# Attention and a two-layer product on one core: earlier dues on VectorE for two pairs, Newton roots for two more, and first-product tiles issued in two parts

## Chip, cores, metric

One core of a Trainium2 chip. The metric is the device time of one execution in microseconds (us), with the median over several runs. "Ratio" below is the mean time of one kernel's fast runs over that of the other kernel's fast runs of the same rounds, so it is not quite the ratio of the medians quoted beside it. All runs here are of state fast. Among them there are still two clusters: some have a mean granted TensorE clock of 0.998 or more, some of 0.991 to 0.997, and the second are longer by 1.2 to 2.2 us (medians) in every kernel that had both. The profiles of e5, e6, x1, x2 and x3 below fell in the second cluster: in each the granted clock was 0.50 for 3.4 us somewhere between 9 and 23 us, ahead of the first half tile, and in none of the other profiles. Half the clock for 3.4 us loses some 1.7 us (an estimate from these figures), which is about the distance of the clusters. Where it matters I give the median of the runs at 0.998 and above ("full clock").

## The reference, cut

```python
def _attn_ref(q, k, v, tau):                       # 8 batches, 12 heads, 448 tokens, 64 wide, fp32
    q_n = q / (norm(q) + 1e-06)
    k_n = k / (norm(k) + 1e-06)
    scores = q_n @ k_n.T / tau                     # tau = 0.1
    attn = softmax(scores)
    return attn @ v
def _moe_ref(x, w_in, w_out):                      # x: 3584 x 768, w_in: 768 x 2048, w_out: 2048 x 768
    h = x @ w_in
    g = h * sigmoid(1.702 * h)
    return g @ w_out
```

Heads are handled in pairs: 6 pairs a batch, 48 in all, numbered through. Batch 0 is pairs 0 to 5, batch 1 is pairs 6 to 11.

## The kernel before

The kernel doesn't issue instructions in program order. Each step ("op") is added to a plan with an engine, an estimated duration, a due, what it must follow, and the buffers it takes and frees. A greedy list scheduler then plays the plan through with those estimates and fixes the order of every engine for good:

```python
def order(self):
    ...
    while True:
        for e in idle:                                   # each engine that is free now
            while idle[e] <= now and ready[e]:
                due, i = heapq.heappop(ready[e])         # the ready op with the smallest due
                ...
                if any(self.free[s] < k ... for s, k in takes):   # a buffer is missing: hold it
                    held.append((due, i)); continue
                ...
                idle[e] = now + us
```

So any change of a due, of a duration or of a group redraws the order of everything after it. The parts that the change touches:

```python
groups = [(x,) for x in range(HP)]                       # HP = 6, PW = 10, HALF = 12
groups += [(x,) for x in range(HP, PW)] + [tuple(range(PW, HALF))] * (PW < HALF)
groups += [tuple(range(g, g + GRP)) for g in range(HALF, NPAIR, GRP)]
...
if x == grp[0] and x in range(HP, PW):                   # pairs 6..9: power 0.5 on GpSimd, inverse on VectorE
    add(("norm", 0, grp), "POOL", 0.5 + 2.4 * n, early + 0.3, partial(power, grp), after=reds)
    add(("norm", 1, grp), "DVE", 0.45, early + 0.3, partial(inverse, grp), after=[("norm", 0, grp)], **port)
elif x == grp[0] and not first:                          # pairs 10 on: Newton steps on VectorE
    add(("norm", 0, grp), "DVE", 0.78 + 0.06 * n, early + 0.3, partial(norm_a, grp), after=reds, **port)
    add(("norm", 1, grp), "DVE", 1.14 + 0.18 * n, early + 0.3, partial(norm_b, grp), after=[("norm", 0, grp)], **port)
...
# batches 0 and 1, by halves h of the queries: attention, normalise, transpose, copy
add(("at", x, h), "PE", 0.48, sh + 1, partial(attend_h, x, h), ..., takes=[("mm", 1), ("run", 1)], ...)
add(("nx", x, h), "DVE", 0.65, sh + 1 - (0 if first else URGENT), partial(normalise_h, x, h), after=[("at", x, h)], ...)
add(("turn", x, h), "PE", 0.15, sh + 1, partial(turn_h, x, h), after=[("nx", x, h)], ...)
add(("x", x, h), ..., "DVE", 0.35, sh + 1 - (0 if first else URGENT), partial(turned_h, x, h), after=[("turn", x, h)],
    ..., frees=[("mm", 1)], ...)
...
def mm1(b, m):                                           # a whole tile of the first product: 6 matmuls, one PSUM bank
    ps = mms[b, m] = bank((b, m))
    for kk in range(KT1):
        nc.tensor.matmul(out=ps[:, :S], lhsT=w_in_sb[:, kk, 128 * m : 128 * (m + 1)], rhs=xTs[b, kk][:, :S], ...)
```

There are three PSUM banks ("mm") for half-batch attention outputs, first-product tiles and second-product tiles together. Batch 0's first product runs in half tiles: 8 for the first half of its tokens, 8 for the second, and the second 8 need the second half of all six pairs. Line numbers: L484 attention product by halves, L507 transpose, L495 and L497 normalise, L517 copy, L581 half tiles of the first product (L583 after the change), L534 whole tiles (L535), L611 second product (L613), L326 power on GpSimd, L343 scaling of queries and keys, L269 reductions, L375 fillers (transposes of the identity whose result nothing reads, put where the plan leaves TensorE idle in the first 50 us).

Of the kernel before, what the change touches and what calls it, by code (L numbers as in the profile page):

```python
# [24 lines left out]
LATE_FROM, LATE_US, URGENT = 80.0, 2.0, 12  # L25
# [5 lines left out]
def packets(n, nbytes):  # L31

    one = DMA_PKT_US + DMA_KB_US * nbytes / 1024
    return n * one / DMA_ENGINES, one
# [8 lines left out]
class Plan:  # L43
# [7 lines left out]
    def add(self, name, eng, us, due, emit, after=(), takes=(), frees=(), dma=None, rows=128, hold=(), turn=False, banks=()):  # L51
        after = list(after) + list(hold)
        if turn:
            self.turns.append((due, len(self.turns), name))
        self.ops[name] = (eng, us, due, emit, after, takes, frees, dma, rows, hold, banks)
# [114 lines left out]
def kernel(  # L170
# [12 lines left out]
    B, H, S, D = q.shape  # L183
# [4 lines left out]
    HP = H // 2  # L188
# [2 lines left out]
    NV, NE = 6, 8  # L191
    NQK = 7
    HALF = 2 * HP
    AHEAD = 3
    LAG, JOINT = (0, 1, 1, 2, 2, 2, 2, 2), 3
    SQP, SQT, XA, CA, TA = range(15, NPAIR), (0,), (), (0, 1, 6), ()
    TURN = 2 * HP
    PW = 10
    SD = ((0, 0), (0, 1), (5, 0), (5, 1))
    SH = S // 2  # L200
    inv_tau = float(1.0 / tau)
# [2 lines left out]
    KT1 = DM // 128  # L204
# [319 lines left out]
    def bank(key):  # L524
        i = plan.bank[key]
        return ps_m.tile([128, 512], FP32, name=f"mm{i}", tag=f"m{i}")


    mms, ths, osts = {}, {}, {}

    def mm1(b, m):
        ps = mms[b, m] = bank((b, m))
        for kk in range(KT1):
            nc.tensor.matmul(  # L534
                out=ps[:, :S],  # L535
                lhsT=w_in_sb[:, kk, 128 * m : 128 * (m + 1)],
                rhs=xTs[b, kk][:, :S],
                start=(kk == 0),
                stop=(kk == KT1 - 1),
            )  # L540
# [33 lines left out]
            op1=ALU.mult,  # L574
        )

    def mm1_h(h, m):
        ps = mms[h, m, "h"] = bank((h, m, "h"))
        for i in range(2):
            for kk in range(KT1):  # L580
                nc.tensor.matmul(  # L581
                    out=ps[:, i * SH : (i + 1) * SH],
                    lhsT=w_in_sb[:, kk, 128 * (m + i) : 128 * (m + i + 1)],  # L583
                    rhs=xTs[0, kk][:, h * SH : (h + 1) * SH],
                    start=(kk == 0),
                    stop=(kk == KT1 - 1),
                )
# [76 lines left out]
    add = plan.add  # L664
    port = dict(takes=[("port", 1)], frees=[("port", 1)])
    groups = [(x,) for x in range(HP)]
    groups += [(x,) for x in range(HP, PW)] + [tuple(range(PW, HALF))] * (PW < HALF)
    groups += [tuple(range(g, g + GRP)) for g in range(HALF, NPAIR, GRP)]
    group_of = {x: g for g in groups for x in g}
    PAIR = packets(2 * P, C * D * 4)  # L670
# [1 line left out]
    def due_of(x):  # L672
        return x if x < HP else 2 * x

    with_mm1 = {}
    for b in range(JOINT, B):
        for i in range(HP):
            x = (b + 1) * HP + LAG[b] + i
# [3 lines left out]
    for x in range(NPAIR):  # L682
        s, grp, first = due_of(x), group_of[x], x < HP
        early = due_of(grp[0]) - (4 if first else 8)
        hold = [("w_in", int(x >= HP + 3))] if HP <= x < 2 * HP else [("w_out", 1)] if x == 2 * HP else []
        for ti, nm in ((1, "k"), (0, "q")):
            add(("load", nm, x), "SP", 0.5, s - 13, partial(load, x, (q32, k32)[ti], (q, k)[ti], nm + "32"),
                takes=[(nm, 1)], dma=PAIR, hold=hold, turn=True)
            pl = sq_pool(x, ti)
            add(("sq", ti, x), "POOL" if pl else "ACT", 1.0 if pl else 0.53, early + ti * 0.1, partial(square, x, ti),  # L690
                after=[("load", nm, x)], takes=[("sq", 1), ("port", int(pl))], frees=[("port", int(pl))])
            add(("red", ti, x), "DVE", 0.6, early + 0.2, partial(reduce, x, ti),
                after=[("sq", ti, x)], frees=[("sq", 1)])
# [3 lines left out]
                after=[("norm", 1, grp)], takes=[("qks", 1), ("port", 1)], frees=[(nm, 1), ("port", 1)])  # L697
        if x == grp[0]:
            reds = [("red", ti, y) for y in grp for ti in range(2)]
            n = len(grp)  # L700
            if first:
                add(("norm", 0, grp), "ACT", 0.48, early + 0.3, partial(root, grp), after=reds)
                add(("norm", 1, grp), "DVE", 0.45, early + 0.3, partial(inverse, grp), after=[("norm", 0, grp)], **port)
        if x == grp[0] and x in range(HP, PW):
            add(("norm", 0, grp), "POOL", 0.5 + 2.4 * n, early + 0.3, partial(power, grp), after=reds)
            add(("norm", 1, grp), "DVE", 0.45, early + 0.3, partial(inverse, grp), after=[("norm", 0, grp)], **port)
        elif x == grp[0] and not first:
            add(("norm", 0, grp), "DVE", 0.78 + 0.06 * n, early + 0.3, partial(norm_a, grp), after=reds, **port)
            add(("norm", 1, grp), "DVE", 1.14 + 0.18 * n, early + 0.3, partial(norm_b, grp), after=[("norm", 0, grp)], **port)
        add(("load", "v", x), "SP", 0.5, s - 9, partial(load, x, v32, v, "v32"),  # L710
            takes=[("v", 1)], dma=PAIR, hold=hold, turn=True)
        ca = x in CA
        add(("cast", x), "ACT" if ca else "POOL", 0.64 if ca else 0.75, s - 0.5, partial(cast_v, x),
            after=[("load", "v", x)], takes=[("vt", 1), ("port", 1 - ca)], frees=[("v", 1), ("port", 1 - ca)])
        if x < TURN:
            add(("tp", x), "PE", 0.4, s - 3, partial(transposes, x),
                after=[("scale", 0, x), ("scale", 1, x)], takes=[("a", 1), ("qkT", 1)], frees=[("qks", 2)])
            add(("qkT", x), "ACT" if x in TA else "DVE", 0.8 if x in TA else 0.6, s - 3, partial(transposed, x), after=[("tp", x)], frees=[("a", 1)])
        else:
            add(("qkT", x), "SP", 1.3, s - 3, partial(dma_transposed, x),  # L720
                after=[("scale", 0, x), ("scale", 1, x)], takes=[("qkT", 1)], frees=[("qks", 2)],
                dma=packets(2 * P, C * D * 4))
        if x < HALF:
            for h in range(2):
                sh = x + HP * h if first else s + h
                for u in range(2):
                    key = (x, h, u)
                    add(("s",) + key, "PE", 0.2, sh, partial(scores_h, *key), after=[("qkT", x)] + [("s", min(x + AHEAD, HP - 1), 0, 1)] * (first and h),
                        takes=[("sp", 1)], frees=[("qkT", h * u)], rows=64)
                    add(("exp",) + key, "ACT", 0.82, sh + 0.1, partial(exp, *key), after=[("s",) + key],  # L730
                        takes=[("exp", 1)], frees=[("sp", 1)])
                es = [("exp", x, h, u) for u in range(2)] + [("cast", x)]
                add(("at", x, h), "PE", 0.48, sh + 1, partial(attend_h, x, h), after=es,
                    takes=[("mm", 1), ("run", 1)], frees=[("exp", 2), ("vt", h)], banks=[(x, h, "x")])
                add(("nx", x, h), "DVE", 0.65, sh + 1 - (0 if first else URGENT), partial(normalise_h, x, h), after=[("at", x, h)],
                    takes=[("xs", 1)])
                add(("turn", x, h), "PE", 0.15, sh + 1, partial(turn_h, x, h), after=[("nx", x, h)],
                    frees=[("xs", 1), ("run", 1)])
                add(("x", x, h), "ACT" if x in XA and not h else "DVE", 0.35, sh + 1 - (0 if first else URGENT), partial(turned_h, x, h), after=[("turn", x, h)],
                    takes=[("x", 1 - h)], frees=[("mm", 1)], banks=[(x, h, "x")])  # L740
            continue
        if x in with_mm1:
            b, m = with_mm1[x]
# [4 lines left out]
            for i, step in enumerate(steps):  # L748
                after = [steps[i - 1]] if i else [("qkT", x)] + [("x", y) + h for y in range(b * HP, (b + 1) * HP) for h in ([(0,), (1,)] if y < HALF else [()])]
                if step[0] == "s":  # L750
                    c = step[2]
                    add(step, "PE", 0.19, s - URGENT * (i > 0), partial(scores, x, c, 1), after=after,
                        takes=[("sp", 1)] + [("mm", 2), ("run", 2), (f"g{b % 2}", 2)] * (i == 0), frees=[("qkT", int(c == C - 1))], rows=64,
                        banks=[(b, m), (b, m + 1)] * (i == 0))
# [3 lines left out]
        for c in range(C):  # L758
            if c % 2 == 0 and x not in with_mm1:
                add(("s", x, c), "PE", 0.38, s + c // 2, partial(scores, x, c), after=[("qkT", x)],  # L760
                    takes=[("sp", 2)], frees=[("qkT", c // 2)], rows=64)
            add(("exp", x, c), "ACT", 0.82, s + c // 2 + 0.1, partial(exp, x, c),
                after=[("s", x, c if x in with_mm1 else c // 2 * 2)], takes=[("exp", 1)], frees=[("sp", 1)])
        for j in range(2):
            es = [("exp", x, c) for c in range(C)] + [("cast", x)]
            if j == 1:
                es.append(("nx", x, 0))
            add(("at", x, j), "PE", 0.475, s + 2 + j, partial(attend, x, j), after=es,
                takes=[("a", 1)], frees=[("exp", 4 * j), ("vt", j)])
            add(("nx", x, j), "DVE", 0.55, s + 2 + j - URGENT, partial(normalise, x, j), after=[("at", x, j)],  # L770
                takes=[("xf", 1 - j)], frees=[("a", 1)])
        add(("x", x), "SP", 1.0, s + 4, partial(turn, x), after=[("nx", x, 1)],
            takes=[("x", 1)], frees=[("xf", 1)], dma=packets(256, 512))
# [3 lines left out]
    def mm1_op(b, u, due, frees):  # L777
        key = u if b else u + ("h",)
        half, m = not b, u[1]
        after = []  # L780
        if half:
            after += [("x", x, u[0]) for x in range(HP)]
        else:
            after += [("x", x) + h for x in range(b * HP, (b + 1) * HP) for h in ([(0,), (1,)] if x < HALF else [()])]
        if b == 0:
            after.append(("w_in", m // 8))
        name = ("mm1",) + key
        if b and (b, m // 2 * 2) in paired:
            name = ("mm1", b, m // 2 * 2, 1)
        else:  # L790
            add(name, "PE", 1.134, due, partial(mm1_h if half else mm1, *u), after=after, takes=[("mm", 1), ("run", 1), (f"g{b % 2}", 1)], frees=[*frees, ("run", 1)],
                banks=[key])
        add(("th",) + key, "ACT", 0.46, due - URGENT, partial(tanh, *key), after=[name], takes=[("th", 1)])
        add(("g",) + key, "DVE", 0.54, due - URGENT, partial(gate_h if half else gate, *u), after=[("th",) + key],
            frees=[("th", 1), ("mm", 1)], banks=[key])
# [32 lines left out]
    for b in range(B):  # L828
# [4 lines left out]
        for u in units:  # L833
            i = solo.index(u) if u in solo else 0
            last = u == units[-1]
# [3 lines left out]
        for i, (t, n) in enumerate(parts):  # L839
            last = n == len(cuts(b // 2, t)) - 1  # L840
            frees = [("g0", KT2 * (last and t == 3)), ("g1", KT2 * (last and t == 6))]
# [58 lines left out]
```

## Time and profile before

| | before |
|---|---|
| median, us | 432.92 (6 runs, 431.46 to 433.29) |
| profiled span, us | 430.0 |
| TensorE busy | 98% |
| TensorE fillers | 238 |
| powers on GpSimd (L326) | 4 |

The page's busy line and the stretch from 46 to 52 us on TensorE and VectorE are in the prediction. What it does not show is GpSimd after it. This is GpSimd's timeline of the kernel before (start, duration, engine, line, operation, count, and in brackets idle time and what ended it):

```profile
51.61 1.05 POOL L343 TENSOR_TENSOR qks<-q,yv 112x512 f16<-112x512 f32 x1
52.61 2.92 POOL L326 TENSOR_TENSOR n<-n,root_of 112x16 f32<-112x16 f32 x1
55.51 1.03 POOL L343 TENSOR_TENSOR qks<-k,yv 112x512 f16<-112x512 f32 x1
56.51 2.89 POOL L326 TENSOR_TENSOR n<-n,root_of 112x16 f32<-112x16 f32 x1
59.38 1.03 POOL L343 TENSOR_TENSOR qks<-q,yv 112x512 f16<-112x512 f32 x1
...
67.63 1.04 POOL L343 TENSOR_TENSOR qks<-q,yv 112x512 f16<-112x512 f32 x1 [0.79 <-DVE y L299]
```

Two powers of 2.9 us stand between the scalings of pair 6 and pair 7, and inside pair 7's. Pair 9 is scaled only at 67.6. And ScalarE, which has 24 exponentials to do for batch 1, is a third idle meanwhile. From the windows view (busy time of PE, PEld, DVE, ACT, POOL in the stretch):

```profile
58.00:65.00 7.00, 6.88 (x95) 6.26 (x95) 5.87 (x16) 4.61 (x9) 6.50 (x10) 1.00 1.28 198
```

### The profile page before, as it was taken

To read this page: it belongs to the slowest core of one execution; us is meant where nothing else is said; L and a number is where in the kernel's file an instruction comes from. 1 tells how busy PE (TensorE), PEld (TensorE's weight loads), DVE (VectorE), ACT (ScalarE), POOL (GpSimd) and SP (SyncE) were. 2 spreads that over 40 slices of the span, in tenths; PEclk is the share of its full clock that TensorE was granted. 3 is DMA by queue.
4 is the path that set the end of the run, shared out by engine and by line. 5 is a ranking of instruction groups with operands and counts; after the bars stand their busy time and mean duration, and the time that the engine had idled before them with its cause. 6 is when DMAs were issued, how large, how long until landed. Compare 5 with 4: busy or idle time off the path is not lost.

```text
span 430.0 us, 11091 instructions
## 1 busy us (share of the span) xinstructions
PE 419.9 (98%) x4438; PEld 261.2 (61%) x4438; DVE 236.5 (55%) x621; ACT 290.5 (68%) x460; POOL 175.4 (41%) x229
## 2 busy tenths in 40 slices
PE   7889999999999999999999999999999999999996
PEld 7768886654565555555556556556656556555564
DVE  5875887877874577829656554553432433123200
ACT  5979679958877788887884886766673864233321
POOL 0830995297678847463682717260100000000000
PEclk9999999999999999999999999999999999999999
DMA  8999997968999999696979475845203021211122
GB/s 215 197 202 268 246 204 207 291 128 203 207 201 184 249 236 204 160 196 169 162 197 220 123 201 134 152 107 93 63 14 93 9 63 49 50 38 37 38 73 75
DMA packets 98099, 64.03 MB, mean 149 GB/s; under 512 B 56320, under 2 KB 93056, under 8 KB 98048
## 3 DMA queue, kind: packets, MB, share of 16 engines
q1 hardware_dynamic: 92320, 57.03, 58.2%
q0 software_dynamic: 5696, 6.29, 8.9%
q8 instruction: 35, 0.57, 0.5%
q14 instruction: 16, 0.13, 0.1%
q10 hardware_dynamic: 32, 0.01, 0.0%
HBM read 45.61 MB, written 11.01 MB: 132 GB/s over the span
## 4 chain that ended last, share of the span: by engine, by line
PE 86%; ACT 4%; DVE 3%; issue 2%; POOL 2%; DMA 1%; SPq 0%; ACTq 0%; POOLq 0%
PE mm L611 34%; PE mm L534 17%; PE mm L552 11%; PE avp L431 8%; PE sp L405 7%; PE sp L467 2%; PE mm L484 2%; ACT et L416 2%; PE mm L581 2%; DMA k<-in_k_dram 1%; ACT sq L263 1%; DVE n L269 1%; POOL qks L343 1%; PE tps L375 1%; POOL n L326 1%
## 5 line engine op out<-in xcount | busy, mean ns | idle before, releaser
L416 ACT ACTIVATE et<-sp 112x896 f16<-112x896 f32 x192 | 170.1, 919 | 29.7 <-PE sp L405 24.8
L611 PE MATMUL mm<-w_out,gT 128*128 128x384 f16 (+1 forms) x912 | 158.4, 323 | 0.0
L611 PEld LDWEIGHTS <-gT 128*128 128x128 f16 x912 | 83.9, 98 | 60.6 <-issue 11.0
L568 DVE SCALAR_TENSOR_TENSOR gT<-th,mm 128x448 f16<-128x448 f16 x112 | 67.0, 616 | 64.9 <-ACT th L563 64.8
L563 ACT ACTIVATE th<-mm 128x448 f16<-128x448 f32 x128 | 67.7, 550 | 39.3 <-PE mm L534 31.9
L534 PE MATMUL mm<-xT,w_in 128*128 128x448 f16 x408 | 85.2, 353 | 0.3 <-DVE gT L568 0.3
L269 DVE TENSOR_REDUCE n<-sq 112x8 f32<-112x512 f32 x96 | 63.9, 679 | 21.8 <-ACT sq L263 13.2
L623 ACT ACTIVATE ost<-mm 128x384 f32<-128x384 f32 (+1 forms) x57 | 27.8, 488 | 62.1 <-PE mm L611 61.7
L534 PEld LDWEIGHTS <-w_in 128*128 128x128 f16 x408 | 37.7, 98 | 36.8 <-issue 5.8
L552 PE MATMUL mm<-xT,w_in 64*128 64x448 f16 x528 | 57.1, 349 | 0.0
L359 POOL CAST vt<-v 112x256 f16<-112x256 f32 x90 | 34.0, 404 | 56.4 <-PE avp L431 42.2
L431 PEld LDWEIGHTS <-et 112*128 112x128 f16 x1152 | 43.6, 97 | 13.8 <-issue 3.7
L343 POOL TENSOR_TENSOR qks<-k,y 112x512 f16<-112x512 f32 x38 | 39.7, 1044 | 26.3 <-DVE y L310 12.9
L431 PE MATMUL avp<-vt,et 112*128 112x65 f16 x1152 | 47.0, 193 | 0.1
L442 DVE RECIPROCAL rcx<-avp 128x4 f32<-128x4 f32 x72 | 13.0, 180 | 61.7 <-PE avp L431 61.6
L262 POOL TENSOR_TENSOR sq<-q 112x512 f32<-112x512 f32 x33 | 34.2, 1041 | 29.4 <-DVE y L310 9.0
L405 PE MATMUL sp<-qkT 64*128 64x448 f16 x288 | 43.3, 353 | 0.0
L343 POOL TENSOR_TENSOR qks<-q,y 112x512 f16<-112x512 f32 x38 | 39.7, 1044 | 0.0
L552 PEld LDWEIGHTS <-w_in 64*128 64x128 f16 x528 | 25.6, 94 | 21.0
L263 ACT ACTIVATE sq<-k 112x512 f32<-112x512 f32 x48 | 30.3, 635 | 3.4 <-DMA k<-in_k_dram 3.4
L445 DVE TENSOR_TENSOR xf<-avp,rcx 128x256 f16<-128x256 f32 x72 | 30.6, 425 | 2.5
L405 PEld LDWEIGHTS <-qkT 64*128 64x128 f16 x288 | 13.4, 93 | 14.6 <-issue 6.7
(48 smaller groups left out, 277.6 us busy)
## 6 DMA issues: line engine op xcount, KB each, us to landing
k<-in_k_dram SPq DMA_DIRECT2D x48, 224.0 KB, 4.5
q<-in_q_dram SPq DMA_DIRECT2D x48, 224.0 KB, 5.0
v<-in_v_dram SPq DMA_DIRECT2D x48, 224.0 KB, 4.2
w_in<-in_moe_w_in_dram POOLq DMA_DIRECT2D x2, 1536.0 KB, 15.7
w_out<-in_moe_w_out_dram POOLq DMA_DIRECT2D x2, 1536.0 KB, 15.4
out_dram<-ost SPq DMA_DIRECT2D x7, 336.0 KB, 4.7
out_dram<-ost SPq DMA_DIRECT2D x8, 288.0 KB, 2.9
out_dram<-ost SPq DMA_DIRECT2D x8, 240.0 KB, 3.1
```

Of the source, the lines that this page charges most:

```text
L262: return nc.gpsimd.tensor_tensor(out=sqs[x, ti], in0=src, in1=src, op=ALU.mult)
L263: return nc.scalar.activation(out=sqs[x, ti], in_=src, func=AF.Square)
L269: nc.vector.tensor_reduce(out=n2s[grp][:, x - grp[0], ti], in_=sqs.pop((x, ti)), axis=AX.X, op=ALU.add,)
L343: return eng.tensor_tensor(out=qkss[x][:, 1 - ti].rearrange("p c j d -> p j c d"), in0=src, in1=rss[x][:, ti, :, :, None].to_broadcast((P, ...
L405: nc.tensor.matmul(out=sp[:, j, :S], lhsT=keys(x, j, c), rhs=queries(x, j, 0, S), start=True, stop=True,)
L416: nc.scalar.activation(out=e[:, : 2 * S].rearrange("p (j s) -> p j s", j=2), in_=sps.pop(key)[:P, :, :S], func=AF.Exp, scale=inv_tau, **kw,)
L431: nc.tensor.matmul(out=ps[:, (D + 1) * t : (D + 1) * (t + 1)], lhsT=exps[x, c][:, q0 : q0 + 128], rhs=values(x, c, D * j, D * j + D + 1), ...
L534: nc.tensor.matmul(out=ps[:, :S], lhsT=w_in_sb[:, kk, 128 * m : 128 * (m + 1)], rhs=xTs[b, kk][:, :S], start=(kk == 0), stop=(kk == KT1 - 1),)
L552: insts.append(nc.tensor.matmul(out=mms[b, m + i][:, :S], lhsT=w_in_sb[rows, kk, 128 * (m + i) : 128 * (m + i + 1)], rhs=xTs[b, kk][rows, :S],
L563: nc.scalar.activation(out=ths[key], in_=mms[key][:, :S], func=AF.Tanh, scale=0.851)
L568: nc.vector.scalar_tensor_tensor(out=gT[:, m, (b % 2) * S : (b % 2 + 1) * S], in0=ths.pop((b, m)), scalar=1.0, in1=mms.pop((b, m))[:, :S], ...
L611: nc.tensor.matmul(out=mms[b2, t, n][:, : c1 - c0], lhsT=gT[:, kk, 128 * t : 128 * (t + 1)], rhs=w_out_sb[:, kk, c0:c1], start=(kk == 0), ...
```

## The change

Three parts. (1) The normalisation and copy of pairs 4 and 5, second half, get a due 12 smaller, so that they pass reductions and gates on VectorE. (2) Pairs 8 and 9 become one group whose roots are Newton steps on VectorE instead of powers on GpSimd. (3) Whole tiles of the first product (not the half tiles) are two ops of three matmuls, between which the scheduler may put other work.

```diff
-    AHEAD = 3
+    AHEAD, PARTS, PU = 3, (2, 1), 0
...
-    PW = 10
+    PW = (6, 7)
...
-    def mm1(b, m):
-        ps = mms[b, m] = bank((b, m))
-        for kk in range(KT1):
+    def mm1(b, m, part, cut):
+        if part == 0:
+            mms[b, m] = bank((b, m))
+        for kk in range(KT1 * part // cut, KT1 * (part + 1) // cut):
... (mm1_h in the same way)
-    groups += [(x,) for x in range(HP, PW)] + [tuple(range(PW, HALF))] * (PW < HALF)
+    groups += [(6,), (7,), (8, 9), (10, 11)]
...
-        if x == grp[0] and x in range(HP, PW):
+        if x == grp[0] and x in PW:
...
-                add(("nx", x, h), "DVE", 0.65, sh + 1 - (0 if first else URGENT), partial(normalise_h, x, h), ...
+                add(("nx", x, h), "DVE", 0.65, sh + 1 - (0 if first and not (h and x >= HP - 2) else URGENT), partial(normalise_h, x, h), ...
... (the copy "x" in the same way)
-            add(name, "PE", 1.134, due, partial(mm1_h if half else mm1, *u), after=after, ...)
+            cut = PARTS[half]
+            for part in range(cut):
+                last = part == cut - 1
+                step = name if last else name + ("part", part)
+                add(step, "PE", 1.134 / cut, due - URGENT * (part > 0) * PU, partial(mm1_h if half else mm1, *u, part, cut), ...)
```

More of the change, by code (lines that the diff above doesn't have):

```diff
@@ L529 @@
     mms, ths, osts = {}, {}, {}
-    def mm1(b, m):
-        ps = mms[b, m] = bank((b, m))
-        for kk in range(KT1):
+    def mm1(b, m, part, cut):
+        if part == 0:
+            mms[b, m] = bank((b, m))
+        for kk in range(KT1 * part // cut, KT1 * (part + 1) // cut):
             nc.tensor.matmul(
-                out=ps[:, :S],
+                out=mms[b, m][:, :S],
                 lhsT=w_in_sb[:, kk, 128 * m : 128 * (m + 1)],
@@ L575, in gate, with mm1_h @@
         )
-    def mm1_h(h, m):
-        ps = mms[h, m, "h"] = bank((h, m, "h"))
-        for i in range(2):
+    def mm1_h(h, m, part, cut):
+        if part == 0:
+            mms[h, m, "h"] = bank((h, m, "h"))
+        for i in range(2 * part // cut, 2 * (part + 1) // cut):
             for kk in range(KT1):
                 nc.tensor.matmul(
-                    out=ps[:, i * SH : (i + 1) * SH],
+                    out=mms[h, m, "h"][:, i * SH : (i + 1) * SH],
                     lhsT=w_in_sb[:, kk, 128 * (m + i) : 128 * (m + i + 1)],
@@ L734 @@
                     takes=[("mm", 1), ("run", 1)], frees=[("exp", 2), ("vt", h)], banks=[(x, h, "x")])
-                add(("nx", x, h), "DVE", 0.65, sh + 1 - (0 if first else URGENT), partial(normalise_h, x, h), after=[("at", x, h)],
+                add(("nx", x, h), "DVE", 0.65, sh + 1 - (0 if first and not (h and x >= HP - 2) else URGENT), partial(normalise_h, x, h), after=[("at", x, h)],
                     takes=[("xs", 1)])
@@ L738 @@
                     frees=[("xs", 1), ("run", 1)])
-                add(("x", x, h), "ACT" if x in XA and not h else "DVE", 0.35, sh + 1 - (0 if first else URGENT), partial(turned_h, x, h), after=[("turn", x, h)],
+                add(("x", x, h), "ACT" if x in XA and not h else "DVE", 0.35, sh + 1 - (0 if first and not (h and x >= HP - 2) else URGENT), partial(turned_h, x, h), after=[("turn", x, h)],
                     takes=[("x", 1 - h)], frees=[("mm", 1)], banks=[(x, h, "x")])
@@ L790, in mm1_op @@
         else:
-            add(name, "PE", 1.134, due, partial(mm1_h if half else mm1, *u), after=after, takes=[("mm", 1), ("run", 1), (f"g{b % 2}", 1)], frees=[*frees, ("run", 1)],
-                banks=[key])
+            cut = PARTS[half]
+            for part in range(cut):
+                last = part == cut - 1
+                step = name if last else name + ("part", part)
+                add(step, "PE", 1.134 / cut, due - URGENT * (part > 0) * PU, partial(mm1_h if half else mm1, *u, part, cut), after=after if part == 0 else [name + ("part", part - 1)],
+                    takes=[("mm", 1), ("run", 1), (f"g{b % 2}", 1)] * (part == 0), frees=[*frees, ("run", 1)] * last, banks=[key])
         add(("th",) + key, "ACT", 0.46, due - URGENT, partial(tanh, *key), after=[name], takes=[("th", 1)])
```

## The prediction

> **What bounds the kernel now.** I read the page first, then the windows, then the engines' timelines from 33 to 91 us, the waits last. The page's own busy lines say where not to look.
>
> ```profile
> PE 419.9 (98%) x4438; PEld 261.2 (61%) x4438; DVE 236.5 (55%) x621; ACT 290.5 (68%) x460; POOL 175.4 (41%) x229
> ```
>
> TensorE is busy 98% and nothing else is near. But that figure counts the fillers of L375 (238 transposes of the identity that only keep the clock up) and says nothing of pace. So I took TensorE's timeline from 51 to 405 us, and for each piece the distance from its start to the next start, less what its matmuls need at the pace of the long unbroken pieces. That pace: 128x448 in 0.189 us (1.134 / 6), 128x384 in 0.1625 (2.60 / 16), half tiles of 224 columns in 0.096, the attention products of 65 columns in 0.030 (0.48 / 16); score matmuls and split tiles on 64 rows run two at a time, so half of 0.189 each. The sum: 341.5 us of pure streaming and 12.9 us left over in 354 us. There are 138 changes between 64-row and 128-row work in it, and nearly all of the rest lies at them (attention product to scores: 31 changes, 3.15 us, so 0.10 us each). The largest true stall is 0.32 us. **From 51 us on the kernel is TensorE streaming end to end**: what is ordered differently there is worth almost nothing, unless the number of mode changes moves. After 405 us the last second-product tiles run unbroken, 144 matmuls, and a short store ends it.
>
> So what can be won lies before 51 us, where TensorE has fillers or gaps. The first 33 us are loads, roots and exponentials of batch 0, which the change leaves alone. Between 33 and 51 us TensorE's timeline has this:
>
> ```profile
> 46.24 0.65 PE L484 MATMUL mm<-vt,et 112*128 112x65 f16 x16
> 46.73 0.33 PE L375 MATMUL tps<-ident 128*128 128x128 f16 x3
> 47.27 1.31 PE L581 MATMUL mm<-xT,w_in 128*128 128x224 f16 x12 [0.20 <-DVE gT L591]
> 48.41 2.29 PE L375 MATMUL tps<-ident 128*128 128x128 f16 x38
> 50.66 0.27 PE L507 MATMUL mm<-ident,xs 112*128 112x112 f16 x2
> 50.77 0.44 PE L375 MATMUL tps<-ident 128*128 128x128 f16 x5
> 51.05 1.31 PE L581 MATMUL mm<-xT,w_in 128*128 128x224 f16 x12
> ```
>
> At 46.24 the last attention product of batch 0 (pair 5, second half) runs, ending about 46.9. Its transpose (L507) comes only at 50.66, and the first half tile of the second half of batch 0 (L581) at 51.05, because it needs the second halves of all six pairs. In between 38 fillers take 2.25 us. VectorE's timeline shows why:
>
> ```profile
> 46.65 0.56 DVE L591 SCALAR_TENSOR_TENSOR gT<-th,mm 128x448 f16<-128x448 f16 x1
> 47.13 0.67 DVE L269 TENSOR_REDUCE n<-sq 112x8 f32<-112x512 f32 x1
> 47.72 0.61 DVE L591 SCALAR_TENSOR_TENSOR gT<-th,mm 128x448 f16<-128x448 f16 x1
> 48.25 1.27 DVE L269 TENSOR_REDUCE n<-sq 112x8 f32<-112x512 f32 x2
> 49.44 0.61 DVE L591 SCALAR_TENSOR_TENSOR gT<-th,mm 128x448 f16<-128x448 f16 x1
> 49.97 0.18 DVE L495 RECIPROCAL rch<-mm 112x4 f32<-112x4 f32 x1
> 50.18 0.42 DVE L497 TENSOR_TENSOR xs<-mm,rch 112x256 f16<-112x256 f32 x1
> 50.97 0.28 DVE L517 COPY xT<-mm 128x224 f16<-128x224 f16 x1 [0.37 <-PE mm L507]
> ```
>
> The normalisation (L495, L497) stands behind gates and reductions that have an earlier due, so it starts 3.1 us after its input is there. Pair 4 has the same in small: attention done by 41.8, normalised at 43.88, its PSUM bank given back only after the copy at 45.56. There are three such banks, and the half tiles at 45.10 and 47.27 had waited for one (0.42 and 0.54 us of filler and gap ahead of them).
>
> **What the Trainium skill says.** (1) "TensorE: Matmul & The Clock Gate", section Back-to-back issue gap, gives N / 2.4 + 2.5 ns: 189.2 ns for 448 columns and 162.5 for 384; the trace's 189 and 162.5 agree, so these stretches have no pace left to win. (The same section puts the sustained spacing for 512 columns at about 131 ns; this trace shows nothing that fast.) (2) "TensorEngine Tiling (Array Packing)", section Key Properties: changing the tiling mode drains TensorE. The trace agrees, at 0.10 us a change. (3) "Perfetto Trace Analysis", section Optimizing Scalar/DVE Operations: GpSimd and VectorE share a port that some VectorE operations hold as a lock. The trace agrees: the tensor_scalar L333 on 16 columns takes 0.17 us alone, but 1.01 at 55.57, ending just as GpSimd's scaling of 55.51 to 56.54 ends.
>
> **The change, part by part.**
>
> *Pairs 4 and 5, second half, first on VectorE.* Their normalisation and copy get a due 12 smaller and so pass the reductions and gates. Pair 4: ready at 41.8, on VectorE at about 42.3, when the running instruction ends, instead of 43.88; its bank comes back near 44.0 instead of 45.8. That should take most of the 0.42 and 0.54 us ahead of the half tiles at 45.10 and 47.27: I take 0.6. Pair 5: its second exponential ends at 45.55 on ScalarE (44.60 + 0.95), which the change doesn't touch, so its attention product still ends about 46.2 to 46.9. Then normalise 0.6 us, wait for the half tile that TensorE has begun (to about 48.0 in the moved schedule, 48.4 in the old), transpose 0.1, copy 0.27 and semaphores 0.1: the second half's first tile at 48.4 to 48.9 instead of 51.05. The hole of 2.25 + 0.28 us shrinks to some 0.4: 2.1 us. The two together: 0.6 + 2.1 = 2.7 us, all of it on the path, since TensorE has had no slack since then. The displaced gates move by 0.6 us each, and half tiles waiting on them can give back 0.2.
>
> *Roots of pairs 8 and 9.* Off GpSimd go two of the four powers of L326, 2.92 us each: 5.8 us, in a stretch (51 to 66 us) where GpSimd is busy 13.7 of 15 us and the chain of waits runs through it. The scaling of pairs 7 to 9 comes up to 5.8 us earlier. On VectorE two pairs of small operations go (2 x (0.39 + 0.25) = 1.3 us) and ten come, at the times that pairs 10 and 11 show: 0.71 (with a lock wait, 0.2 without) + 6 x 0.19 + 0.18 + 0.35 + 0.19 = 2.1 to 2.6 us. So VectorE gains about 1.0 us, where it is busy 12.3 of 15 us. For the time: TensorE in 51 to 66 us has only some 1 us of gaps and switches (0.31 and 0.28 at transposes that came just after a scaling). I give this part 0.2 us itself; its worth is that work is there when the half tiles come 2.5 us earlier.
>
> *Whole tiles in two parts.* The 68 whole tiles (408 matmuls of L534, 6 each) may be cut after the third matmul. No matmul is added: 3 x 0.189 twice is the same 1.134. Scores then wait for TensorE at most 0.57 us instead of 1.13. But ScalarE, which they feed, isn't the bound after 91 us, and the number of score groups is the same, so about the same 138 changes. Worth 0, uncertain by 0.6 either way (six changes more or fewer).
>
> Sum: 2.7 - 0.2 + 0.2 + 0 = 2.7 us; 432.85 - 2.7 = 430.15, and as parts one and two can only add a little more in the 33 to 51 us stretch I say **430.0 us**.
>
> **The rivals.** (a) *The hole is hidden by another wait.* Pair 5 may then wait for its bank, or the tiles for gates held up by the normalisation. For: the tiles at 45.10 and 47.27 did wait for gates, and VectorE is busy 13.75 of 18 us there. Against: VectorE's bulk is reductions, which nothing on TensorE needs for some us. It would leave 1 us of gain: 431.8. (b) *GpSimd is the true bound from 42 to 61 us.* For: the chain of waits passes through its powers, w_out issues and scalings. Against: TensorE is streaming meanwhile and stalls under 1 us; a chain follows one last releaser at each step and not the amount of work. If true, 5.8 us off GpSimd would make up to 3 us more: 427. (c) *The cut tiles scatter the 64-row work.* More score groups in pieces, 20 changes more at 0.10 us: 2 us lost, 432. For: the schedule is built greedily, and a small shift reorders all that follows. Against: scores are already issued in groups as small as their two buffers allow. (d) *Newton on VectorE delays the gates* of the second half's tiles, each up to 1 us, with three banks: perhaps 0.5 us back.
>
> **Range and chances.** The three runs of before span 1.1 us. The gain's core, 2.1 us, is a hole seen in the trace; (a) and (c) pull to 432, (b) to 427.5. I take 427.8 to 432.0 as eight in ten. Faster by over 2% needs 424.2, and the whole of the gaps between 33 and 51 us is 5 us: 0.03. Slower by over 2% needs some 90 more mode changes or a broken schedule: 0.01. Within 2%: 0.96.
>
> **What would show it.** Right: the run of 38 fillers is gone, the second half's first half tile starts near 48.5, L495 and L497 of pairs 4 and 5 follow their attention products within 0.6 us, fillers fall from 238 to about 195; the powers are two, the Newton rows on 32 columns double; the time from the first tile of the second half to the end stays about 379 us; mode changes from there to the last tile stay 130 to 145. Wrong: the first tile starts near 48.5 but the end doesn't follow (then rival c or d), or new gaps over 0.5 us after it, or a gain over 4 us with TensorE's later stretch shortened.

## The result, and the profile after

The changed kernel takes 428.8 us (median of 6, 428.0 to 430.35) against 432.92: ratio 0.9918, 95% interval 0.9892 to 0.9944. That is 4.1 us by the medians and 3.7 by the profiled spans (430.0 and 426.3). The predicted 430.0 us and range hold. The page after the change:

```profile
PE 416.5 (98%) x4404; PEld 258.2 (61%) x4404; DVE 236.3 (55%) x627; ACT 291.6 (68%) x460; POOL 169.7 (40%) x227
```

TensorE has 34 instructions less, all fillers (238 to 204). GpSimd is 5.7 us less busy. VectorE, for all its new small operations, is where it was. TensorE's timeline where the hole was:

```profile
45.12 0.65 PE L484 MATMUL mm<-vt,et 112*128 112x65 f16 x16
45.61 0.78 PE L375 MATMUL tps<-ident 128*128 128x128 f16 x11
46.63 0.27 PE L507 MATMUL mm<-ident,xs 112*128 112x112 f16 x2 [0.24 <-DVE xs L497]
46.74 0.28 PE L375 MATMUL tps<-ident 128*128 128x128 f16 x2
47.15 4.76 PE L583 MATMUL mm<-xT,w_in 128*128 128x224 f16 x48
```

The attention product of the last pair is followed by 11 fillers, not 38, and the half tiles run on from 47.15. What is left of the hole is on VectorE:

```profile
45.08 0.71 DVE L333 TENSOR_SCALAR yv<-n 112x16 f32<-112x16 f32 x1
45.82 0.25 DVE L334 RECIPROCAL yv<-yv 112x16 f32<-112x16 f32 x1
45.99 0.12 DVE L495 RECIPROCAL rch<-mm 112x4 f32<-112x4 f32 x1
46.15 0.42 DVE L497 TENSOR_TENSOR xs<-mm,rch 112x256 f16<-112x256 f32 x1
```

An inverse (L333) was issued just before the normalisation. It lasted 0.71 us and ended as GpSimd finished issuing a weight load (44.57 to 45.81); at 51.91 in the same trace it took 0.17. And GpSimd later:

```profile
50.95 1.04 POOL L343 TENSOR_TENSOR qks<-q,yv 112x512 f16<-112x512 f32 x1
51.94 1.44 POOL L359 CAST vt<-v 112x256 f16<-112x256 f32 x4
53.34 1.03 POOL L343 TENSOR_TENSOR qks<-k,yv 112x512 f16<-112x512 f32 x1
54.34 1.04 POOL L343 TENSOR_TENSOR qks<-q,yv 112x512 f16<-112x512 f32 x1
...
62.16 1.04 POOL L343 TENSOR_TENSOR qks<-q,y 112x512 f16<-112x512 f32 x1
```

Pair 7 is scaled by 55.4 instead of 60.4, pair 9 by 63.2 instead of 68.7. ScalarE is fed in the same window:

```profile
58.00:65.00 7.00, 7.00 (x111) 5.36 (x109) 6.53 (x18) 6.54 (x10) 4.75 (x6) 1.00 1.20 187
```

6.54 us busy instead of 4.61.

**Where the 3.7 us went.** I use one account for all kernels. TensorE's timeline is cut at the first half tile of batch 0 and at the start of the last unbroken run of the second product. Between them, TensorE needs 349.6 to 350.1 us of streaming at the paces that the prediction gives. The matmuls are the same in every kernel, so the spread of 0.5 us is the account's own error, and differences of stalls below that say nothing. What is over lies at changes between 64-row and 128-row work, or elsewhere (fillers and stalls).

| us | before | after |
|---|---|---|
| start of the first half tile | 33.15 | 32.49 |
| first half tile to last run | 372.21 | 369.19 |
| of it at mode changes | 15.19 (146) | 15.19 (146) |
| of it fillers and stalls, to batch 0's last transpose and the fillers behind it | 4.29 | 2.20 |
| of it fillers and stalls later | 2.97 | 1.80 |
| last transpose of batch 1, from the first half tile | 56.86 | 54.20 |

So 0.66 us came ahead of the first half tile, where TensorE's order is the same in both kernels and the fillers that wait for the first loads took 7.87 us in one profile and 6.99 in the other: that is chance of the first loads, not the change. 3.0 us came after it: 2.1 out of the stretch to the last transpose, and some 0.9 out of later stalls (3.02 less 2.09; the row says 1.2, within the account's error). The last row says that batch 1's attention ended 2.7 us earlier. In the experiments below, the kernels with 54.2 in this row are the fast ones; among those with 56 to 57 the time varies by 3 us, so the row alone does not give the time.

### The profile page after: what moved, and what is told of

It reads as the page before. It is cut to its first block, busy times and chain, and to the rows that moved or that the text cites. A ratio compares the mean times of both kernels' runs of the same rounds, so it can differ in the third digit from the quotient of the medians.

```text
span 426.3 us, 11033 instructions
## 1 busy us (share of the span) xinstructions
PE 416.5 (98%) x4404; PEld 258.2 (61%) x4404; DVE 236.3 (55%) x627; ACT 291.6 (68%) x460; POOL 169.7 (40%) x227
## 3 DMA queue, kind: packets, MB, share of 16 engines
q1 hardware_dynamic: 92320, 57.03, 58.7%
## 4 chain that ended last, share of the span: by engine, by line
PE 89%; DVE 4%; ACT 3%; issue 1%; DMA 1%; SPq 0%; DVEq 0%; ACTq 0%
PE mm L613 35%; PE mm L535 19%; PE mm L553 11%; PE avp L431 8%; PE sp L405 7%; PE mm L583 3%; PE mm L484 2%; PE sp L467 2%; ACT et L416 2%; DVE n L269 1%; DMA k<-in_k_dram 1%; ACT sq L263 1%; PE tps L367 1%; PE tps L375 1%; DVE gT L593 1%
## 5 line engine op out<-in xcount | busy, mean ns | idle before, releaser
L416 ACT ACTIVATE et<-sp 112x896 f16<-112x896 f32 x192 | 170.9, 920 | 32.7 <-PE sp L405 27.9
L564 ACT ACTIVATE th<-mm 128x448 f16<-128x448 f32 x128 | 67.6, 549 | 32.2 <-PE mm L535 27.9
L625 ACT ACTIVATE ost<-mm 128x384 f32<-128x384 f32 (+1 forms) x57 | 27.9, 489 | 62.0 <-PE mm L613 61.8
L343 POOL TENSOR_TENSOR qks<-k,y 112x512 f16<-112x512 f32 x40 | 41.8, 1044 | 21.7 <-issue 11.6
L442 DVE RECIPROCAL rcx<-avp 128x4 f32<-128x4 f32 x72 | 13.0, 180 | 62.6 <-PE avp L431 62.4
L343 POOL TENSOR_TENSOR qks<-q,y 112x512 f16<-112x512 f32 x40 | 41.8, 1044 | 0.8 <-DVE y L299 0.8
```

The lines of the kernel that those rows point to most:

```text
L343: return eng.tensor_tensor(out=qkss[x][:, 1 - ti].rearrange("p c j d -> p j c d"), in0=src, in1=rss[x][:, ti, :, :, None].to_broadcast((P, ...
L416: nc.scalar.activation(out=e[:, : 2 * S].rearrange("p (j s) -> p j s", j=2), in_=sps.pop(key)[:P, :, :S], func=AF.Exp, scale=inv_tau, **kw,)
L564: nc.scalar.activation(out=ths[key], in_=mms[key][:, :S], func=AF.Tanh, scale=0.851)
```

## The experiments

All twelve ran with five rounds. The first four had these theories. **Theory 1**, the prediction's: the hole ahead of batch 0's second half is the gain. **Rival G**: GpSimd bounds 42 to 61 us, and the roots are the gain. **Rival P**: the cut tiles save later stalls. After them I formed two others. **Theory S**: the earlier start is kept only if the pairs of batch 1 are supplied earlier too, since the end of their attention is the later of two limits. **Theory L**: the redrawn order after any change moves the time by 1 to 2 us with no cause in the part.

In the table, "last b0" and "last b1" are the last transpose of batch 0 and of batch 1, and "run" the start of the last run of the second product, all from the first half tile; "stalls" are those after the last transpose of batch 0 and the fillers behind it; all from one profiled execution each. The profile of x3 had a second stretch of 3.4 us at half clock, from 62.4 to 65.8 us, so some 1.7 us in its row (an estimate) is not in its full-clock runs. The median is of the runs at full clock, with their number. The full-clock median of the kernel before was 431.91 (4), 431.66 (38) and 431.64 (27) in the rounds of the three batches of experiments.

| kernel | due | roots | cut | ratio (95%) | full clock | last b0 | last b1 | run | mode changes | stalls |
|---|---|---|---|---|---|---|---|---|---|---|
| before | | | | | 431.66 (38) | 17.51 | 56.86 | 372.21 | 146 | 2.97 |
| e1_only_due | x | | | 1.0004 (0.9987 to 1.0020) | 432.43 (5) | 14.16 | 57.03 | 373.07 | 152 | 5.01 |
| e2_only_roots | | x | | 0.9988 (0.9970 to 1.0006) | 431.66 (4) | 17.52 | 57.27 | 372.06 | 150 | 2.80 |
| e3_only_parts | | | x | 1.0029 (1.0007 to 1.0050) | 433.55 (4) | 17.53 | 56.87 | 373.27 | 148 | 3.8 |
| e4_no_parts | x | x | | 0.9943 (0.9930 to 0.9956) | 430.15 (6) | 14.16 | 54.22 | 370.40 | 148 | 2.78 |
| e5_no_roots | x | | x | 1.0018 (1.0006 to 1.0030) | 432.66 (15) | 14.15 | 57.02 | 373.08 | 150 | 5.17 |
| e6_no_due | | x | x | 0.9985 (0.9972 to 0.9999) | 431.41 (15) | 17.51 | 57.26 | 371.59 | 150 | 2.10 |
| after | x | x | x | 0.9918 (0.9892 to 0.9944) | 428.48 (4) | 14.14 | 54.20 | 369.19 | 146 | 1.80 |
| p1_redraw_before | | | | 1.0015 (1.0002 to 1.0028) | 432.23 (15) | 17.51 | 56.35 | 372.81 | 150 | 3.03 |
| p2_redraw_after | x | x | x | 0.9941 (0.9919 to 0.9963) | 428.75 (2) | 14.14 | 54.20 | 369.04 | 144 | 1.71 |
| p3_redraw_no_parts | x | x | | 0.9941 (0.9920 to 0.9963) | 429.15 (6) | 14.14 | 54.20 | 369.90 | 150 | 1.97 |
| x1_powers_back | x | x | x | 0.9999 (0.9983 to 1.0016) | 431.12 (8) | 14.17 | 56.11 | 371.81 | 146 | 4.15 |
| x2_all_newton | x | x+ | x | 0.9970 (0.9954 to 0.9986) | 430.52 (17) | 14.08 | 56.07 | 371.09 | 152 | 3.4 |
| x3_newton_exp | x | x+ | x | 1.0044 (1.0021 to 1.0068) | 433.41 (7) | 13.23 | 60.48 | 375.40 | 152 | 8.0 |

Every result was correct.

### Each part alone: e1_only_due, e2_only_roots, e3_only_parts

```diff
 e1: PARTS = (1, 1); groups (6,), (7,), (8,), (9,), (10, 11); PW = (6, 7, 8, 9)
 e2: PARTS = (1, 1); due of "nx" and "x" as before
 e3: groups, PW and dues as before
```

> Only the earlier due of pairs 4 and 5 (second half), roots and tiles as before. Theory 1 (the hole of fillers ahead of the second half's first tile is the gain): 2 to 3 us faster than before, ratio 0.993 to 0.995; the ninth half tile starts within 15.5 us of the first (17.9 before) and the fillers fall from 238 to about 205. Rival G (GpSimd bounds 42 to 61 us, so the roots are the gain): under 1 us faster, as the powers are still there. Rival P (the cut tiles are the gain): under 1 us.

> Only pairs 8 and 9 by Newton steps. Theory 1: within 0.6 us of before, ratio 0.9985 to 1.0015; 238 fillers and the ninth half tile 17 to 18 us after the first, though GpSimd is 5.8 us less busy. Rival G: 2 us or more faster.

> Only the whole tiles issued in two parts. Theory 1: within 0.6 us of before, up to 33 us and on to the ninth half tile the same trace; mode changes after it 132 to 144. Rival P: 1 to 1.5 us faster, from stalls outside mode changes after 51 us (2.96 us before, 1.80 with the whole change).

The first of these was a miss, and the most useful run of the study. The hole closed exactly as in the whole change (last transpose of batch 0 at 14.16 us from the first half tile, 204 fillers), and yet the kernel was no faster: ratio 1.0004. (A slip in the expectations: the tile 14.7 us after the first, which they call the ninth, is the first one behind the hole, and is the eighth; the ninth starts 15.83 us after the first here and 15.81 in the changed kernel, against 17.90 before.) GpSimd had its powers still:

```profile
52.42 2.92 POOL L326 TENSOR_TENSOR n<-n,root_of 112x16 f32<-112x16 f32 x1
55.32 1.03 POOL L343 TENSOR_TENSOR qks<-k,yv 112x512 f16<-112x512 f32 x1
56.32 2.89 POOL L326 TENSOR_TENSOR n<-n,root_of 112x16 f32<-112x16 f32 x1
59.18 1.03 POOL L343 TENSOR_TENSOR qks<-q,yv 112x512 f16<-112x512 f32 x1
```

Pair 7 is scaled no earlier than before, ScalarE was busy 5.08 us in the window from 58 to 65 (4.61 before, 6.54 after), and batch 1's attention ended 57.0 us after the first half tile, as before. TensorE spent the time it had won on second-product tiles of batch 0, which it has to do anyhow: 80 of their matmuls were issued before batch 1's last transpose, against 68 in the kernel before and in the changed one. Those 12 matmuls of 0.1625 us are 2.0 us. When batch 1's attention ended late, few of those were left beside the whole tiles of batch 1, and it stalled. TensorE's timeline of e1_only_due:

```profile
91.85 2.11 PE L613 MATMUL mm<-w_out,gT 128*128 128x384 f16 x12
93.80 1.30 PE L535 MATMUL mm<-xT,w_in 128*128 128x448 f16 x6
96.39 4.70 PE L535 MATMUL mm<-xT,w_in 128*128 128x448 f16 x24 [1.29 <-DVE gT L569]
```

and ScalarE's:

```profile
95.14 0.54 ACT L564 ACTIVATE th<-mm 128x448 f16<-128x448 f32 x1 [2.02 <-PE mm L535]
95.58 0.87 ACT L625 ACTIVATE ost<-mm 128x384 f32<-128x384 f32 x2
```

As I read it, all three banks were taken: one by the tile that TensorE had just finished, two by second-product results whose evictions (L625) stood in ScalarE's fixed order behind that tile's tanh (L564). TensorE waited 1.45 us beyond the tile's streaming for the gate, until 96.39. Two stalls of 0.78 us at 201 and 214 us and six more mode changes took the rest.

The roots alone do nothing measurable (0.9988), though GpSimd's 5.8 us are gone: TensorE then comes late to the pairs because of the hole, and batch 1's attention ends at 57.27. The distances between the two last transposes fit that: 39.8 us here and 40.1 in the changed kernel, but 42.9 with the due alone. So rival G in its plain form falls too. The cut alone is slightly slower (1.0029), which neither theory 1 (within 0.6 us) nor rival P (faster) had asked for: the trace up to the ninth half tile is the one of before, and one stall of 0.79 us at 204 us came in.

### Two parts at a time: e4_no_parts, e5_no_roots, e6_no_due

```diff
 e4: PARTS = (1, 1)
 e5: groups (6,), (7,), (8,), (9,), (10, 11); PW = (6, 7, 8, 9)
 e6: due of "nx" and "x" as before
```

> Earlier due and roots, whole tiles in one part. Theory 1: as the whole change within 0.6 us, ratio to before 0.990 to 0.994. Rival P: 1 to 1.5 us slower than the whole change, ratio about 0.995.

> Whole change without the Newton roots (earlier due and cut tiles). Both theories: ninth half tile 14.7 us after the first. Theory S (the earlier start is kept only if GpSimd is freed, as otherwise the next batch's pairs come too late and TensorE stalls later): same as before within 1 us, ratio 0.998 to 1.002, with a stall of over 1 us between 85 and 100 us as when the due was changed alone. Theory L (what follows is a redrawn static order whose stalls and mode changes vary by 1 to 2 us with no cause in the part): anything from 0.990 to 1.000, and no stall of over 1 us need be there.

> Whole change without the earlier due (roots and cut tiles). Both theories: hole of 38 fillers and 17.9 us from first to ninth half tile are back, so 2.1 us slower than the whole change plus or minus what the later order does. Theory S: ratio to before 0.996 to 1.000. Theory L: 0.994 to 1.003.

Only the pair of due and roots gains: e4_no_parts 0.9943, against 1.0018 and 0.9985. In e5_no_roots the stall of 1.45 us was there again, until 98.45 us, at the same place of the work as in e1_only_due (its first half tile started 2.1 us later), which theory S had asked for and theory L had not. Its profile also has 1.5 us of waits inside an attention product at 230 to 231 us, with no counterpart in e1_only_due, so its 5.17 us of stalls are not all due to the part. The roots alone and the due alone each leave batch 1's attention at 57 us; both together bring it to 54.2. So it looks not like a sum of two gains but like the later of two limits; x1_powers_back below tests that.

e4_no_parts lacks some of the whole change's gain. Its largest later stall, on its TensorE timeline:

```profile
189.52 0.82 PE L613 MATMUL mm<-w_out,gT 128*128 128x384 f16 x4
190.94 1.30 PE L535 MATMUL mm<-xT,w_in 128*128 128x448 f16 x6 [0.61 <-DVE gT L569]
```

Four matmuls of 0.1625 us end by 190.2; the whole tile then waits for a bank until the first gate of the tile pair ahead is done, at 190.9. In the changed kernel another order falls here and no such stall.

### Nothing changed but the draw: p1_redraw_before, p2_redraw_after, p3_redraw_no_parts

```diff
-            add(("mm2", b2, t, n, part), "PE", 0.652 * (c1 - c0) / NW, ...
+            add(("mm2", b2, t, n, part), "PE", 0.66 * (c1 - c0) / NW, ...
```

This is an estimate that only the scheduler reads, put into the kernel before (p1), the changed one (p2) and e4_no_parts (p3).

> The kernel before with one estimate of the scheduler changed that no engine sees (four matmuls of the second product 0.66 us instead of 0.652), so nothing changes until some 66 us and the order is redrawn after it. Theory S: no change, ratio 0.9985 to 1.0015, stalls outside mode changes after the last transpose of batch 0 within 0.5 us of the 2.97 us of before. Theory L: the time moves by 0.5 to 1.5 us either way, with stalls or mode changes to match.

> The changed kernel with the same blind change of one estimate. Theory S: ratio as the changed kernel, 0.990 to 0.9935. Theory L: moves by 0.5 to 1.5 us, more likely slower, as the changed kernel's 1.8 us of later stalls are the least seen so far.

> Earlier due and roots, whole tiles in one part, with the blind change of one estimate (0.66 for 0.652). If cutting the tiles is what took away the stall of 0.77 us at 189.5 us: the stall is there again, ratio 0.9935 to 0.9955. If it was the draw: with even chances the stall is gone and the ratio is 0.990 to 0.993.

At full clock p1 is 0.6 us slower than before, p2 is 0.3 us from the changed kernel (two runs only; its ratio of 0.9941 comes from four runs of the lower clock among six), and p3 1.0 us faster than e4_no_parts (0.7 us, each against the kernel before of its own rounds), whose stall of 0.77 us is gone without any cut. So a redraw alone moved the time by up to about 1 us in these three, and theory L holds for that size, not for the 1.8 to 3.2 us (at full clock) of the pair of due and roots: a gain of that size came in all four draws that have both as the change sets them, and in none without. The nearest of the others, x2_all_newton below, gained 1.1 us.

What the cut of the whole tiles is worth can't be told from a redraw. With both other parts there are two draws with it (428.48, 428.75) and two without (430.15, 429.15); alone it lost 1.6 us at full clock against before (four runs, two near 432.6 and two near 434.5). It stays open.

### GpSimd's time put back: x1_powers_back

```diff
+    scratch = const.tile([P, 16], FP32, name="scratch")
+    nc.vector.memset(scratch, 1.0)
+    def idle_power(x):
+        return nc.gpsimd.tensor_tensor(out=scratch, in0=scratch, in1=root_of.to_broadcast((P, 16)), op=ALU.pow)
...
+            if x == 8:
+                for y in (8, 9):
+                    add(("idle", y), "POOL", 2.9, due_of(y) - 8 + 0.3, partial(idle_power, y), after=[("red", ti, y) for ti in range(2)])
```

> The whole change, with two powers on GpSimd put back that compute nothing used (a scratch tile), ahead of pair 7's scaling where the old ones stood; the roots stay Newton steps on VectorE. Theory S (the end of batch 1's attention is the later of two limits, TensorE's hole and GpSimd's scalings): the last transpose of batch 1 goes back from 54.2 us to about 57 us after the first half tile, and the time goes back to 431.5 to 433, ratio 0.998 to 1.002. Theory L (a redrawn order only): the last transpose stays at 54 to 55 and the ratio at 0.990 to 0.995.

This is the direct test: everything of the change stays, the Newton steps too, and GpSimd's time comes back (5.9 us; one small memset is new as well). GpSimd's timeline:

```profile
54.34 1.04 POOL L351 TENSOR_TENSOR qks<-q,yv 112x512 f16<-112x512 f32 x1
55.34 5.90 POOL L334 TENSOR_TENSOR scratch<-scratch,root_of 112x16 f32<-112x16 f32 x2
61.20 1.04 POOL L351 TENSOR_TENSOR qks<-k,yv 112x512 f16<-112x512 f32 x1
```

Nearly the whole gain went: ratio 0.9999, and at full clock 431.12 us against 431.64 before and 428.48 with the change, so 2.6 of 3.2 us. Batch 1's attention ended at 56.1 us (theory S had said about 57, theory L 54 to 55). TensorE stood waiting for GpSimd's scalings of pair 7 at 62.3 and 63.3 us, and a stall in front of 99.4 us, as in e1 and e5, was back:

```profile
62.30 0.37 PE L375 MATMUL tps<-ident,qks 112*128 112x112 f16 x4 [0.25 <-POOL qks L351]
63.30 0.37 PE L375 MATMUL tps<-ident,qks 112*128 112x112 f16 x4 [0.63 <-POOL qks L351]
...
97.10 1.30 PE L543 MATMUL mm<-xT,w_in 128*128 128x448 f16 x6
99.41 0.92 PE L543 MATMUL mm<-xT,w_in 128*128 128x448 f16 x4 [1.01 <-ACT ost L633]
```

With that it is shown, not only argued, that the roots pay through GpSimd's time, and that without it the closed hole (14.17 us here too) is worth 0.5 us at most. It is one draw; the 2.6 us are more than the 1 us that a redraw moved. How the later end of batch 1 turns into the stall at 95 to 99 us is read from the traces and was not tested by itself.

### Two tries to go further: x2_all_newton, x3_newton_exp

```diff
 x2: groups (6, 7), (8, 9), (10, 11); PW = ()
 x3: as x2, and the due of the exponentials of pairs 4 and 5, second half, 12 smaller
```

> The whole change, with pairs 6 and 7 by Newton steps as well: no power is left on GpSimd (5.9 us less of it). Theory S, if GpSimd is still the limit: pair 6 is scaled 2 to 4 us earlier and batch 1's attention ends 1 to 2 us earlier, ratio 0.987 to 0.990. If TensorE's half tiles are now the limit: as the changed kernel, 0.990 to 0.9935. If VectorE's 1.5 us more before the last normalisation matter: slower, 0.993 to 0.996.

> As the run with all Newton steps, and the exponentials of pairs 4 and 5, second half, get the earlier due on ScalarE too. If the rest of the hole (1.0 us of fillers ahead of the last transpose of batch 0) comes from ScalarE, it shrinks, and the ninth half tile starts 0.5 to 1 us earlier after the first (14.66 us in the changed kernel); in time 0.5 us at most, as later stalls vary by as much.

Neither beats the change, and neither came out as expected: x2's ratio of 0.9970 lies in none of the three ranges, and x3 is slower where 0.5 us of gain was the most. With no power left, pairs 6 and 7 are scaled no earlier (17.7 us after the first half tile, 17.5 in the changed kernel), the scaling of pairs 10 and 11 comes 1.2 us later, and batch 1's attention ends at 56.1 us; why the last pairs slip I did not find out. It is not GpSimd's work: GpSimd stood idle for 3.25 us before that scaling, and for 1.89 in the changed kernel. In x3_newton_exp the hole did shrink (13.23), but the first exponential of batch 1 slipped from 22.7 to 27.9 us, TensorE stood 2.14 us in front of 61.35, and it was the slowest of all against the kernel before of its rounds. The column "last b1" goes with the time in both.

## Why the prediction was right or wrong

**The time: right.** 430.0 predicted, 428.8 measured, within the range. At full clock the changed kernel took 428.48 (4 runs), and the kernel before 431.64 to 431.91 in other rounds, so some 3.2 to 3.4 us, against 2.85 predicted from the medians. That the number fits is in part luck: of the predicted 2.7 us at the hole 2.1 came, and they count only because the roots freed GpSimd; the rest is later stalls (some 1 us), which the prediction did not have and which are no more than a redraw moves.

**Pairs 4 and 5: the mechanism right, the sizes off.** For pair 4 the prediction took 0.6 us; the filler and gaps ahead of the two half tiles, 0.42 and 0.54 us, went altogether, so 0.96. For pair 5 it took 2.1; the hole of 2.25 + 0.28 us became 1.02 + 0.41, so 1.1. One half tile of the first half now comes after the hole instead of before it, and the inverse L333 ahead of the normalisation took 0.71 us instead of 0.17. Sum 2.1 us against 2.7.

**"All of it on the path, since TensorE has had no slack since then": this step failed.** The reason given was that TensorE streams from 51 us to the end, so that an earlier start moves the end. With the hole alone closed the end did not move at all. The flaw is that a full engine shows only that it had enough to do at the pace of before; it does not show that its suppliers could go faster. Ahead by 2 us, TensorE met the next limit, batch 1's pairs behind GpSimd's powers, and stood 1.45 us in front of 96.39.

**"I give this part 0.2 us itself": mis-sized, but its second clause was right.** The prediction said that the roots' worth "is that work is there when the half tiles come 2.5 us earlier". That is what x1_powers_back shows. But with 0.2 us in the sum the roots looked dispensable, and they decide between nothing and the whole gain. Rival (b), GpSimd as the bound, was argued away with "TensorE is streaming meanwhile", which is the same flaw; as a sole bound it was rightly rejected (e2_only_roots).

**VectorE's cost: right.** The Newton steps took 2.0 us for the two pairs by their durations, with no lock wait (0.17 us for L282), against 2.1 to 2.6 predicted, and rival (d) did not show. "GPSIMD Engine Reference", section Key points, of the Trainium skill says that VectorE is structurally about twice as fast elementwise; here ten VectorE instructions for two pairs took 2.0 us where two powers took 5.8. As these are other operations, that points the same way but does not test the figure.

**The cut: "worth 0, uncertain by 0.6"** is too sure. Mode changes were 146 and 146, as said, but redraws move the time by up to 1 us through bank stalls, which the prediction had not sized: it had looked at mode changes alone. Later stalls fell by 0.9 to 1.2 us in the profile, a part of the gain that the prediction had left at nil.

**Signs:** fillers 204 (195 said), powers two, mode changes as said, normalisations within 0.4 us of their attention products. The first tile of the second half was to start near 48.5: it starts at 48.30, 1.15 us after the tile at 47.15, which still belongs to the first half. "The time from the first tile of the second half to the end stays about 379 us": 426.3 - 48.30 = 378.0, against 430.0 - 51.05 = 378.95 before; the 0.9 us are the later stalls.

## What to carry to other kernels

An engine that is full after a hole is not proof that closing the hole moves the end: ask what its suppliers can deliver when it arrives earlier, and look for the later of two limits, since then each cure alone measures as nothing. Put the suspected cost back into the finished version, as with the two idle powers, rather than only taking parts away. And where a greedy planner fixes the order, redraw it with a blind change before believing any difference under the spread that this shows, here about 1 us.

## What the Trainium skill lacked or had wrong

- "TensorE: Matmul & The Clock Gate", section Back-to-back issue gap: it puts the sustained spacing at about 131 ns for 512 columns and calls N / 2.4 + 2.5 the isolated case that over-counts. Here unbroken runs of weight load and matmul hold 189 ns for 448 columns and 162.5 ns for 384 in every kernel, which is that formula (no matmul here has 512 columns; other parts of the page use the formula for back-to-back matmuls too, so it is this section's 131 that finds no support here). With it and 0.10 us a mode change, all but 4 to 9 us of fillers and stalls in some 370 us is accounted for in every kernel.
- The same page, Part 1 on the clock gate: it says that the clock halves after an idle window of about 3.4 us. In the five profiles of the slower cluster the granted clock fell to 0.50 for 3.4 us at a time, six times in all (twice in x3), though no gap in TensorE's work before these falls was longer than 1.97 us. In e5_no_roots the fillers ended at 8.45 us, and until 12.09 TensorE did about 1.6 us of matmuls with no gap over 1.15 us; the clock fell at about 11.5. What sets it off is not shown: in e6_no_due it fell at about 17.6 us after the same order of work, with gaps of at most 0.74 us, that left it at 1.00 in the kernel before. The windows view of e5_no_roots (TensorE busy, then the clock, the DMA share and GB/s):

```profile
9.00:11.00 2.00, 0.74 (x8) 1.00 1.16 279
11.00:13.00 2.00, 1.67 (x17) 0.62 1.09 277
13.00:15.00 2.00, 2.00 (x23) 0.53 1.12 272
```

- "TensorEngine Tiling (Array Packing)", section Key Properties: it says that a change of tiling mode drains TensorE and gives no figure. Here 0.10 us is left over at a change between 64-row and 128-row work by the account above, 15.2 us over 146.
- "GPSIMD Engine Reference" has no figure for a power: 2.92 us for 112 x 16 fp32 elements, against 1.04 us for a two-input product of 112 x 512.
